# The rounding pass of the weights' high part on GpSimd in place of ScalarE

## The chip, the cores and the metric

One core of a Trainium2 chip runs the whole program: one launch, inputs and output in device memory. The metric is the device time of an execution in microseconds (us). The kernel before took 1209.21 us, the median of three runs (1208.96 to 1211.28).

## The reference

Top-k attention, then two feed-forward layers. All tensors are float32 except the weights, which are float64 (the draw is multiplied by a float64 scalar).

```python
scores = scale * q @ k^T                       # 4 batches, 8 heads, 576 tokens, 64 columns
kth = the 32nd largest of each row of scores
scores = where(scores >= kth, scores, -1e9)
attn = exp(scores - max) / (sum + 1e-9)
x = (attn @ v), heads side by side             # 2304 x 512
h = max(x @ w_in, 0);  x = (h * h) @ w_out     # 512 -> 2048 -> 512
h = x @ w_in2;  out = max(0.01 * h, h) @ w_out2
```

## The kernel before, in words

*Precision by parts.* TensorE multiplies values in a reduced 32-bit format (`R` in the code). To keep float32 accuracy the kernel splits a tensor into a high part, which is the value rounded to that format, and a low part, the value minus the high part. A product is then three matmuls: high by high, high by low, low by high. The helper `split_hi` (L111) makes a high part: with `act=True` on ScalarE, otherwise as one `tensor_scalar` on GpSimd that multiplies by 1.0 twice (L115). The low part is a `tensor_tensor` subtraction.

*Attention.* The 2304 tokens lie in nine units of 64 to 320 tokens; each unit has four head pairs, and the 128-row tiles of all of them go in 72 pairs of tiles through VectorE. For one pair VectorE alternates eight MAX8 (L829) and six MATCH_REPLACE8 (L831) to find the 32 largest of each row; then GpSimd makes the shifts `nb` (L288, L289), ScalarE the mask and the exponentials with their sums (L295, L299), GpSimd and VectorE the reciprocal (L303, L304), GpSimd the scaling of the rows (L308), TensorE the transposes (L313, L326) and the products with v (L397, L408). Score matmuls (L276) are evicted by ScalarE (L277).

*Feed-forward.* The tokens go in six blocks (512, 256, 384, 512, 256, 384). A block goes through a layer in 16 steps, one for each 128 columns of the hidden layer. Each step is 12 matmuls into `h` (L575), then the activation, which yields `gh` and `gl` (high and low part of the hidden values), and 12 matmuls into `acc` (L618 in the first layer, L620 in the second). The `acc` matmuls of a step come after the `h` matmuls of the next one (`LAG = 1`). In the first layer of block 0 the activation is relu and square on ScalarE (L585, L586), then on GpSimd the product L587 and the difference L601. In the second it is two relus on ScalarE (L596, L597), GpSimd's difference L598, ScalarE's `gh` (L600) and GpSimd's `gl` (L601).

*Weights.* A step uses a tile `wi` and a tile `wo`, each with a high and a low half of 128x512. Block 0 meets each of the 2 x 16 steps' weights for the first time and has to make them; it runs between about 180 and 445 us. Later blocks load the finished halves (`w_load`, L537, L538) from a copy in device memory that `w_store` (L529, L530) wrote. Making a tile (`w_convert_steps`): SP loads the raw float64 words (`w_raw`, L486, 4 buffers), ScalarE takes both 32-bit words to a scratch tile `wc` (4 buffers) and to a PSUM bank (L509, L510), VectorE joins them into the float32 value (L514, L515), ScalarE rounds it to the high half (L519), and GpSimd subtracts for the low half (L521). So 64 tiles, each with one L519 and one L521.

*Order.* The program is written out as a list of slots, 16 for each pair of attention tiles; each event (a load, a split, a score matmul) has a slot, and the feed-forward steps advance by portions between them, at a rate fixed for each block. A generator's `yield` ends a portion. While a step's matmuls are emitted, `next(conv, None)` emits one more portion of the conversion of the step after the next (`w_convert(si + 2)`): three times among the `h` matmuls, once behind the activation, four times among the `acc` matmuls; what is left over is emitted at the end of the step. `w_store(si + 1)` and `w_raw(si + 4)` stand at a step's start and end. The framework then orders the instructions by priority (events and conversions have a raised one) against its own model of the engines, puts in the semaphores, and each engine works its queue strictly in that order.

Of the kernel before, what the change touches and what calls it, by code (L numbers as in the profile page):

```python
# [11 lines left out]
AF = mybir.ActivationFunctionType  # L12
# [59 lines left out]
def topk_attention_moe_moe2_kernel(  # L72
# [21 lines left out]
    PE, ACT, DVE, POOL, SP = nc.tensor, nc.scalar, nc.vector, nc.gpsimd, nc.sync  # L94
# [6 lines left out]
    def bank():  # L101
        return psum.tile([P, 512], F, tag="att", name="att", bufs=3)
# [4 lines left out]
    def behind(key):  # L107

        return tc.issue_after(cur[key].ins) if key in cur else ExitStack()

    def split_hi(dst, src, act=False):  # L111
        if act:
            ACT.activation(dst, src, AF.Copy)
            return
        POOL.tensor_scalar(dst, src, 1.0, 1.0, op0=OP.mult, op1=OP.mult)  # L115
# [355 lines left out]
    def w_alloc(i):  # L471
        wi = pool.tile([P, 2, 512], R, tag="wi", name="wi", bufs=3)
        wo = pool.tile([P, 2, 512], R, tag="wo", name="wo", bufs=4)
        wt[i] = (wi, wo)
        return wi, wo
# [16 lines left out]
    def w_convert(i):  # L492
        g = w_convert_steps(i)
        while True:
            with tc.high_priority(offset=CONVP):
                if next(g, 1):
                    return
            yield

    def w_convert_steps(i):  # L500
        if i >= len(steps) or not fresh[i]:
            return
        w2 = w_alloc(i)
        for raw, w in zip(wraw.pop(i), w2):
            if W64:
                lo, hi = raw[:, :, 0], raw[:, :, 1]
                b = pool.tile([P, 512], U, tag="wc", name="wc", bufs=WCB)
                v = bank()
                ACT.activation(b, lo, AF.Copy, scale=L_SCALE, bias=L_BIAS)  # L509
                ACT.activation(v, hi.bitcast(F), AF.Copy, scale=H_SCALE)  # L510
                yield 0
                vu, c = v.bitcast(U), b.bitcast(F)
                with behind("dve"):
                    DVE.scalar_tensor_tensor(b, vu, 3, b, op0=OP.logical_shift_left, op1=OP.bitwise_or)  # L514
                DVE.scalar_tensor_tensor(b, vu, 0x80000000, b, op0=OP.bitwise_and, op1=OP.bitwise_or)  # L515
                yield 0
            else:
                c = raw
            ACT.activation(w[:, 0, :], c, AF.Copy)  # L519
            yield 0  # L520
            POOL.tensor_tensor(w[:, 1, :], c, w.bitcast(F)[:, 0, :], op=OP.subtract)  # L521
            yield 0

# [381 lines left out]
```

## Time and profile before

| what | value |
|---|---|
| median of three runs | 1209.21 us |
| the profiled execution | 1210.15 us, span 1208.4 us |
| TensorE matmul (PE) | busy 1135.8 us, 94% |
| VectorE (DVE) | busy 946.5 us, 78% |
| ScalarE (ACT) | busy 807.5 us, 67% |
| GpSimd (POOL) | busy 682.8 us, 57% |
| mean granted TensorE clock | 0.98 of full speed |

The profile is of one execution. Busy time leaves out register, branch, semaphore and DMA-issuing instructions. PEld is TensorE's weight load, which overlaps the matmuls. Lines (L519) are those of the kernel's file, where a helper's instructions have the helper's line. The shares are means over stretches with different limits, so most of what follows is read from one stretch.

### The profile page before, as it was taken

The page shows a single profiled execution, that of the slowest core. Times are in us where ns is not written, and L with a number is a line of the kernel's source. Part 1 is how long each engine was busy: PE and PEld are TensorE (multiplying, and loading weights), DVE is VectorE, ACT ScalarE, POOL GpSimd, SP SyncE. Part 2 cuts the span into 40 slices and gives each one's busy share as a digit, 9 for nine tenths or more (in the row PEclk, how much of TensorE's full clock was granted, in tenths as well). Part 3 has the DMA queues.
Part 4 walks back from the last instruction along what each step waited for, and adds up shares of the span by engine and source line. Part 5 has one row for each costly group of instructions (what it writes and reads, how often), then busy time and mean ns, then how long its engine had stood idle before and what let it go on. Part 6 is the DMA issues. An engine that isn't in the chain of part 4 may idle for free.

```text
span 1208.4 us, 20261 instructions
## 1 busy us (share of the span) xinstructions
PE 1135.8 (94%) x6388; PEld 992.5 (82%) x6388; DVE 946.5 (78%) x1944; ACT 807.5 (67%) x1831; POOL 682.8 (57%) x982
## 2 busy tenths in 40 slices
PE   4988987999889999999999999999999999999998
PEld 3776765887678779988999898888788899999997
DVE  7999899868988999999999999999999930110122
ACT  6988898878998986766656666555666653334322
POOL 7765564877878876556666665555565644004300
PEclk9899897999999999999999999999999999999999
DMA  9765566779989888879988888776676679779974
GB/s 307 255 217 192 192 220 222 267 233 333 342 280 319 305 267 263 296 269 384 355 293 290 298 272 286 221 227 226 201 239 211 199 255 369 253 253 341 356 256 135
DMA packets 110522, 323.25 MB, mean 268 GB/s; under 512 B 17488, under 2 KB 25680, under 8 KB 110416
## 3 DMA queue, kind: packets, MB, share of 16 engines
q1 hardware_dynamic: 107776, 317.24, 77.5%
q10 hardware_dynamic: 2640, 4.72, 1.1%
q8 instruction: 52, 0.85, 0.3%
q14 instruction: 54, 0.44, 0.1%
HBM read 254.54 MB, written 67.37 MB: 266 GB/s over the span
## 4 chain that ended last, share of the span: by engine, by line
PE 71%; ACT 11%; DVE 7%; DMA 6%; issue 2%; POOL 1%; ACTq 0%; SPq 0%; POOLq 0%; DVEq 0%
PE h L575 29%; PE acc L620 14%; PE acc L618 14%; PE att L408 4%; PE att L313 4%; DVE m L829 3%; PE att L397 3%; DVE w L831 3%; DMA wraw<-in_w_dram 2%; DMA sd<-stage 2%; ACT stage L277 1%; ACT e L299 1%; ACT e L295 1%; ACT s L277 1%; PE sp L276 1%
## 5 line engine op out<-in xcount | busy, mean ns | idle before, releaser
L575 PE MATMUL h<-xh,wi 128*128 128x512 f32 (+2 forms) x1280 | 349.9, 345 | 13.4 <-ACT gb L597 4.2
L829 DVE MAX8 m<-w 128x8 f32<-128x576 f32 x432 | 311.9, 748 | 1.1
L575 PEld LDWEIGHTS h<-xh,wi 128*128 128x128 f32 x1280 | 227.5, 191 | 42.6 <-ACT gb L597 5.8
L831 DVE MATCH_REPLACE8 w<-m,w 128x576 f32<-128x576 f32 x288 | 213.5, 744 | 0.8
L575 PE MATMUL h<-xl,wi 128*128 128x512 f32 (+2 forms) x640 | 207.6, 342 | 0.6 <-DVE xl L632 0.6
L601 POOL TENSOR_TENSOR gl<-ga,gh 128x512 fp32r<-128x512 f32 (+2 forms) x160 | 162.7, 1017 | 37.9 <-ACT gh L600 32.1
L618 PE MATMUL acc<-gh,wo 128*128 128x512 f32 (+2 forms) x768 | 156.8, 340 | 0.0
L620 PE MATMUL acc<-wo,gh 128*128 128x512 f32 x576 | 152.5, 399 | 2.9 <-ACT gh L600 2.7
L598 POOL TENSOR_TENSOR ga<-ga,gb 128x512 f32<-128x512 f32 (+2 forms) x80 | 81.4, 1017 | 130.6 <-ACT gb L597 127.3
L618 PEld LDWEIGHTS acc<-gh,wo 128*128 128x128 f32 x768 | 126.5, 189 | 11.0 <-ACT gh L586 0.2
L575 PEld LDWEIGHTS h<-xl,wi 128*128 128x128 f32 x640 | 121.4, 191 | 12.3 <-DVE xl L632 1.1
L295 ACT ACTIVATE e<-s,m 128x576 f32<-128x576 f32 x144 | 111.7, 779 | 18.6 <-DVE m L829 13.4
L620 PEld LDWEIGHTS acc<-wo,gh 128*128 128x128 f32 x576 | 104.3, 189 | 24.1 <-ACT gh L600 5.0
L829 DVE MAX8 m<-s 128x8 f32<-128x576 f32 x144 | 104.1, 748 | 12.5 <-ACT s L277 6.1
L299 ACT ACTIVATE e<-e,nb 128x576 f32<-128x576 f32 x144 | 111.0, 774 | 3.2 <-POOL nb L289 2.8
L587 POOL TENSOR_TENSOR ga<-ga 128x512 f32<-128x512 f32 (+2 forms) x80 | 66.1, 827 | 78.1 <-ACT gh L586 72.8
L831 DVE MATCH_REPLACE8 w<-m,s 128x576 f32<-128x576 f32 x144 | 107.1, 744 | 0.6
L313 PE MATMUL att<-ident,e 128*128 128x128 f32 x576 | 90.8, 281 | 13.7 <-ACT e L299 5.1
L313 PEld LDWEIGHTS att<-ident,e 128*128 128x128 f32 x576 | 70.0, 143 | 27.4 <-ACT e L299 10.1
L308 POOL TENSOR_SCALAR e<-e,rc 128x576 f32<-128x576 f32 x108 | 79.8, 749 | 22.5 <-DVE rc L304 21.1
L585 ACT ACTIVATE ga<-h 128x512 f32<-128x512 f32 (+2 forms) x80 | 39.0, 488 | 77.4 <-PE h L575 71.9
L618 PE MATMUL acc<-gl,wo 128*128 128x512 f32 (+2 forms) x384 | 87.7, 345 | 0.1
(94 smaller groups left out, 2136.7 us busy)
## 6 DMA issues: line engine op xcount, KB each, us to landing
wi<-wd SPq DMA_DIRECT2D x160, 512.0 KB, 5.0
wo<-wd SPq DMA_DIRECT2D x160, 512.0 KB, 5.2
wraw<-in_w_dram SPq DMA_DIRECT2D x64, 512.0 KB, 6.0
sd<-stage SPq DMA_DIRECT2D x72, 288.0 KB, 2.9
s<-sd SPq DMA_DIRECT2D x72, 288.0 KB, 4.6
wd<-wi SPq DMA_DIRECT2D x32, 512.0 KB, 5.4
wd<-wo SPq DMA_DIRECT2D x32, 512.0 KB, 5.9
kraw<-in_k_dram SPq DMA_DIRECT2D x16, 576.0 KB, 5.4
```

The costliest lines, as they stand in the source:

```text
L295: ACT.activation(t["e"], t["s"], AF.Prelu, bias=pr["m8"][:, i, 31:32], scale=-1.0, alpha=0.125 / FAR)
L299: ACT.activation(e, e, AF.Exp, bias=pr["nb"][:, i:i + 1], scale=-FAR, accum_out=pr["sum"][:, i:i + 1])
L308: POOL.tensor_scalar(e, e, pr["rc"][:, i:i + 1], 1.0, op0=OP.mult, op1=OP.mult)
L313: PE.transpose(ps[:, j * P:(j + 1) * P], t["e"][:, j * P:(j + 1) * P], ident)
L575: PE.matmul(h[:, 0:n], lhsT=wi[:, w, c * P:(c + 1) * P], rhs=x[c][y][:, 0:n], start=cnt == 0, stop=cnt == 3 * NK - 1)
L587: POOL.tensor_tensor(a[:, 0:n], a[:, 0:n], a[:, 0:n], op=OP.mult)
L598: POOL.tensor_tensor(a[:, 0:n], a[:, 0:n], b[:, 0:n], op=OP.subtract)
L601: (DVE if j >= GLD else POOL).tensor_tensor(gl[:, 0:n], a[:, 0:n], gh.bitcast(F)[:, 0:n], op=OP.subtract)
L618: PE.matmul(acc[c][:, 0:n], lhsT=wo[:, w, cs], rhs=g[:, 0:n], start=first, stop=last)
L620: PE.matmul(acc[c], lhsT=g[:, cs], rhs=wo[:, w, :], start=first, stop=last)
L829: cur["dve"] = DVE.max(out=m8[:, x, 8 * r:8 * r + 8], in_=t["s"] if r == 0 else t["w"])
L831: cur["dve"] = DVE.match_replace(out=t["w"], in_to_replace=m8[:, x, 8 * r:8 * r + 8], in_values=t["s"] if r == 0 else t["w"], imm_value=NEG)
```

## The change

The conversion's rounding pass calls the helper, which without `act` uses GpSimd. It stands directly in front of the subtraction that reads its result, and the `yield` between the two is gone, so that a tile's conversion has three portions and a step's six.

```diff
             else:
                 c = raw
-            ACT.activation(w[:, 0, :], c, AF.Copy)
-            yield 0
+            split_hi(w[:, 0, :], c)
             POOL.tensor_tensor(w[:, 1, :], c, w.bitcast(F)[:, 0, :], op=OP.subtract)
             yield 0
```

`split_hi(dst, src)` is `POOL.tensor_scalar(dst, src, 1.0, 1.0, op0=OP.mult, op1=OP.mult)`.

## Rows read from the trace of the kernel before

**Rows 1.** Windows, all engines: stretch, length, busy us (instructions), granted clock, DMA share, GB/s.
```profile
core 0: us, PE busy (x) PEld busy (x) DVE busy (x) ACT busy (x) POOL busy (x), PEclk, DMA share, GB/s
180.00:280.00 100.00, 91.67 (x440) 73.74 (x440) 83.24 (x165) 80.32 (x173) 65.88 (x76) 0.91 0.74 249
280.00:335.00 55.00, 45.35 (x205) 34.91 (x204) 48.41 (x93) 51.31 (x106) 43.49 (x49) 0.97 0.92 336
335.00:437.00 102.00, 99.30 (x479) 81.43 (x480) 89.05 (x166) 92.27 (x187) 88.57 (x92) 0.98 0.87 296
437.00:945.00 508.00, 499.06 (x2913) 445.28 (x2911) 499.77 (x1052) 326.22 (x723) 301.72 (x465) 0.99 0.80 270
945.00:1208.00 263.00, 256.30 (x1561) 240.08 (x1559) 60.66 (x119) 102.07 (x229) 63.88 (x91) 0.99 0.78 270
```
**Rows 2.** Windows, all engines, 280 to 437 us as one stretch.
```profile
280.00:437.00 157.00, 144.65 (x683) 116.34 (x683) 137.46 (x258) 143.58 (x293) 132.06 (x140) 0.98 0.89 310
```
**Rows 3.** Waits of PE, 280 to 437: waiter <- awaited, us, times, longest.
```profile
PE h L575 <- ACT gb L597: 3.4, 3, 2.2
PE h L575 <- ACT wi L519: 3.1, 2, 1.6
PE att L408 <- DVE PTs L336: 2.3, 2, 1.3
PE att L276 <- ACT s L277: 1.5, 1, 1.5
PE acc L620 <- ACT gh L600: 1.3, 1, 1.3
PE h L575 <- ACT ga L585: 0.6, 1, 0.6
```
**Rows 4.** Chain of waits (start us, us, what), and a window with the granted clock.
```profile
283.41 4.60 PE h L575 x12
...
334.96 4.57 PE h L575 x12
...
343.46 2.77 PE h L575 x12
...
284.00:286.00 2.00, 2.00 (x6) 1.52 (x6) 1.99 (x4) 2.00 (x5) 1.07 (x3) 0.50 1.02 416
```
**Rows 5.** ScalarE's line L519, 280 to 437: count, ns min/median/max, first and last start.
```profile
L519 ACT ACTIVATE wo<-wc x22: 616/624/663, 279.4 to 431.5; 128x512 fp32r<-128x512 f32 x22
L519 ACT ACTIVATE wi<-wc x21: 612/618/667, 282.7 to 429.2; 128x512 fp32r<-128x512 f32 x21
its engine sat idle before it (us, times) until:
  DVE wc L515: 1.5, 4
```
**Rows 6.** GpSimd's groups by shape: count | busy us, mean ns | idle before.
```profile
L115 POOL TENSOR_SCALAR q<-qraw 128x320 fp32r<-128x320 f32 x24 | 11.0, 458 | 24.5 <-PE sp L276 22.6 <-PE att L276 1.9
L115 POOL TENSOR_SCALAR KTa<-kraw 128x576 fp32r<-128x576 f32 x16 | 10.4, 670 | 1.9 <-DMA kraw<-in_k_dram 1.9
...
L521 POOL TENSOR_TENSOR wo<-wc,wo 128x512 fp32r<-128x512 f32 x32 | 41.5, 1295 | 5.5 <-ACT wo L519 5.2
```
**Rows 7.** GpSimd's timeline at two places: start us, us, instruction.
```profile
346.44 0.46 POOL L115 TENSOR_SCALAR q<-qraw 128x320 fp32r<-128x320 f32 x1 [0.86 <-PE att L276]
346.99 0.88 POOL L255 TENSOR_TENSOR q<-qraw,q 128x320 fp32r<-128x320 f32 x1
...
371.71 0.48 POOL L115 TENSOR_SCALAR q<-qraw 128x320 fp32r<-128x320 f32 x1
372.14 1.32 POOL L601 TENSOR_TENSOR gl<-ga,gh 128x512 fp32r<-128x512 f32 x1
```
**Rows 8.** Waits of GpSimd, 280 to 437.
```profile
POOL wi L521 <- ACT wi L519: 4.3, 3, 1.9
POOL sum L303 <- ACT e L299: 4.3, 4, 1.7
POOL ga L598 <- ACT gb L597: 3.8, 2, 2.7
POOL gl L601 <- ACT gh L600: 3.6, 4, 1.8
POOL e L308 <- DVE rc L304: 2.5, 4, 1.3
POOL ga L587 <- ACT gh L586: 2.5, 2, 2.2
POOL wo L521 <- ACT wo L519: 2.1, 4, 0.9
POOL q L115 <- PE att L276: 1.0, 2, 0.9
```
**Rows 9.** Waits of SP's DMA queue, 280 to 437.
```profile
SPq L529 <- POOL wi L521: 27.2, 16, 5.2
SPq L530 <- POOL wo L521: 15.2, 13, 3.8
```
**Rows 10.** Waits of VectorE and ScalarE on conversion lines, 280 to 437.
```profile
DVE wc L514 <- ACT att L510: 6.9, 7, 2.8
...
ACT wc L509 <- DMA wraw<-in_w_dram: 3.2, 2, 1.9
```
**Rows 11.** GpSimd's groups by line, 280 to 437.
```profile
L308 POOL TENSOR_SCALAR e<-e,rc 128x576 f32<-128x576 f32 x14 | 10.3, 748 | 2.6 <-DVE rc L304 2.5
L587 POOL TENSOR_TENSOR ga<-ga 128x512 f32<-128x512 f32 x6 | 6.2, 1039 | 2.5 <-ACT gh L586 2.5
```

## The prediction

> **What bounds the kernel now.** I read the profile in four steps: busy time by stretch, who waited for whom on TensorE, how the two engines of the change spend the stretch that has the conversions, and the queue of GpSimd instruction by instruction. All 64 rounding passes and their 64 subtractions lie between 180 and 437 us, so only that stretch can change by itself; everything behind it can only move. Behind it nothing has slack to give back or to soak up: from 437 to 945 VectorE is busy 500 of 508 us and TensorE 499, and from 945 to the end TensorE 256 of 263 [rows 1]. TensorE's whole work is fixed, so a shift of the end is the change of TensorE's idle time up to 437 us.
>
> The conversion stretch has two halves that differ. From 180 to 280 us nothing is full but TensorE, and GpSimd has 34 of 100 us free [rows 1]. From 280 to 437 us TensorE is busy 144.7 and ScalarE 143.6 of 157 us, 92% each, VectorE 88% and GpSimd 132.1, 84% [rows 2]. In its last 102 us TensorE is at 99.3: there it is the bound, with ScalarE (92.3) and GpSimd (88.6) close under it [rows 1]. TensorE's 12.4 us of idle in the 157 us are nearly all waits for ScalarE and VectorE: 3.4 for gb, 3.1 for the rounding pass L519 itself, 2.3 for PTs, 1.5 for a score eviction, 1.3 for gh, 0.6 for ga [rows 3]. After its longer pauses TensorE also runs some matmuls at the lower of its two clocks (granted share 0.50): twelve then take 4.60 and 4.57 us in place of 2.77 [rows 4].
>
> **The change, part by part.** *Removed from ScalarE:* 64 passes of 0.62 us, some 40 us in all; 43 of them between 280 and 437, 26.7 us [rows 5]. ScalarE falls there from 143.6 to 117 of 157 us and stops being near full. What is behind such a pass on its in-order queue comes earlier: the score evictions, relu, gh and the next tensor's two splitting passes.
>
> *Added to GpSimd:* 64 passes of 128x512, one input, from the helper at L115. The trace has this operation at 320 columns (458 ns) and 576 (670 ns) [rows 6]: 0.83 ns a column, so 512 columns take 670 - 64 x 0.83 = 617 ns. What one adds to a full queue is its start-to-start step. Ahead of an independent instruction a 0.48 us pass gave a step of 0.43 (371.71 to 372.14); ahead of the subtraction that needs it a 0.46 us pass gave 0.55 (346.44 to 346.99) [rows 7]. So 0.57 to 0.70 us each; I take 0.62, nearer to the first, because the scheduler may put another instruction between the two. Far bounds: 0.46 us (the 320-column row) and 1.30 us (the two-input row of the same 512 columns, L521) [rows 6]. Sum 64 x 0.62 = 39.7 us, of it 43 x 0.62 = 26.7 between 280 and 437.
>
> The Trainium skill, "GPSIMD Engine Reference", section 3.1, gives 769 ns as measured for 512 elements at its best-case loop of about 1.8 cycles an element, and elsewhere in that section 1.03 cycles for bodies of at most two operations. The rows' slope, 0.83 ns, is 1.0 cycle at the page's 1.2 GHz, so the trace sides with the second; by the first the 43 passes would be 33.1 us, 6.4 more than my sum.
>
> *The sum for GpSimd, 280 to 437:* 132.1 busy now plus 26.7 is 158.8 us of work in a stretch of 157. The earlier half stays under its length: 65.9 + 21 x 0.62 = 78.9 of 100. GpSimd cannot be busy without a gap. Its 24.9 us idle now are 6.4 for L519 itself (3 + 4 times), 14.2 for other ScalarE results (e, gb, gh), 2.5 for the reciprocal and 1.0 for a matmul [rows 8]. The first goes: the pass then waits for VectorE's L515, for which ScalarE idled only 1.5 us here [rows 5]. The reciprocal wait stays, a round trip from GpSimd to VectorE and back, and so does the 1.0: 3.5 us. Of the 14.2 I keep a quarter, 3.5, since a late engine finds its inputs ready and a lighter ScalarE delivers earlier. So 158.8 + 3.5 + 3.5 = 165.8 us for what takes 157: +8.8. Bounds of this term: with no gap and the 0.57 step, 156.6, nothing; with the 0.70 step and 92% busy, the best that any engine reaches in this stretch now, (132.1 + 30.1) / 0.92 = 176, +19.
>
> *What queues behind the added pass:* on GpSimd the products and differences L598 and L601, which release gh (by L600) and the last third of the second matmul group, the shifts nb that release the exponentials, and the sums that release the reciprocal. TensorE waited only 1.3 us for gh here, but it has just one hidden step of lag between the two layers' matmuls. On SP the stores L529 and L530 wait for the subtraction's result already, 27.2 + 15.2 us in this stretch [rows 9]; behind them stand the loads of the next raw weights, for which L509 waited 3.2 us [rows 10]. Each store comes later by what GpSimd is late.
>
> *Moved:* a conversion of two tensors is emitted in six portions, not eight, beside a matmul step that offers eight; so it ends a quarter of a step earlier, and 24 matmuls of 0.23 us (2.77 / 12) make 5.5 us, a quarter 1.4. It hides the pass's own latency, which is why I charge GpSimd's capacity and not its latency; without that cover, and with the subtraction's result needed at once, each step would pay 2 x 0.62.
>
> *Gain ahead of 280 us:* TensorE idles 8.3 us from 180 to 280 [rows 1], 22 rounding passes of ScalarE lie there, and ScalarE is 80% busy. I take 2 us, between 0 and 5.
>
> Net +8.8 - 2 = +6.8. The profiled execution took 1210.15 us (span 1208.4, 1.75 around it), 0.9 over the median of the runs, 1209.21; so 1216.95 for a profile and 1216 for the median. A measurement of this kernel tells 0.2%, 2.4 us, from no change.
>
> **Rivals.** *ScalarE was the pace-maker and its relief wins.* For it: the pass is in TensorE's waits by name (3.1 us), ScalarE's results end 9.9 of the 12.4 us of TensorE's idle in the stretch [rows 3], VectorE waits 6.9 us for L510 [rows 10], and each of two pauses cost another 1.8 us at the lower clock [rows 4]. Price at most 9.9 + 3.6 + 5 ahead of 280 = 18.5; TensorE's 99.3 of 102 leave little in the last part, so some 8: 1201. It decides if GpSimd's gaps shrink to almost nothing, that is if the stretch ends below 157 with GpSimd near 100%. Against it: 158.8 is more than 157.
>
> *No change.* GpSimd runs a few us behind through the stretch but the two-step lead of the weights absorbs it, and TensorE, 97% busy from 335 on, sets the pace as now: 1209.
>
> *The delay multiplies.* GpSimd at 92% as in the bound above, +19, and two more pauses with a lower-clock restart, 3.6, less the 2 ahead: some +17 to +21, 1228. It decides if L598 stands behind rounding and subtraction together (0.62 + 1.30 us), since then gh is late in every step.
>
> *The pass is slower than its helper's rows say.* The other one-input pass of GpSimd, L308, takes 748 ns at 576 columns, so some 0.69 us at 512, and L587, which multiplies a tile by itself, 1.04 us at 512 [rows 11]. At 0.69 the 43 passes add 3.3 us to my sum, at 1.04 18; the first row is much the nearer in kind: 1220. The skill's 769 ns, named above, would give 1222. It decides from the first pass on, and its row against it is L115's own.
>
> *That the change doesn't do what it says:* the scheduler may order the queues afresh, so that products go ahead of conversions; this moves the time either way by a pause or two, 2 to 5 us, and is in the ranges.
>
> **How the numbers follow.** Forecast case (slower by 3 to 13): 0.40. Relief wins: 0.23. No change: 0.20. Multiplied delay: 0.13. Slower pass: 0.04. Slower by over 0.2%: 0.40 + 0.13 + 0.04 = 0.57; within: 0.20; faster: 0.23. For the range I leave out half of the relief case below 1202 and some 0.06 of the multiplied delay above 1227; the forecast's own range is 1212 to 1222.
>
> **What would show it.** In the profile after: L115 with 64 more instructions near 617 ns and no L519 on ScalarE; GpSimd's busy time 39 us higher, ScalarE's 40 lower; GpSimd near 95% between 280 and the end of the conversions, and that end later by 5 to 10 us; TensorE's waits for gh and gl grown, those for s and gb shrunk; behind it the same distances as now. Wrong if the conversions end earlier than 437 us, if GpSimd keeps its gaps with TensorE at its old pace, or if the shift arises behind 437.

## The result and the profile after

The changed kernel takes 1219.91 us, the median of 7 runs (1216.54 to 1224.18), against 1209.50 for the kernel before (7 runs): 0.83% slower, ratio 1.0083, 95% interval 1.0068 to 1.0098. The forecast was 1216 with 1202 to 1227. The profiled execution has a span of 1220.5 us, 12.1 more than before.

The busy times did what the diff says. This is the page's first part for the changed kernel (busy us, share of the span, instructions):

```profile
span 1220.5 us, 20225 instructions
PE 1140.9 (93%) x6388; PEld 995.3 (82%) x6388; DVE 946.4 (78%) x1944; ACT 777.5 (64%) x1767; POOL 720.2 (59%) x1046
```

ScalarE has 64 instructions and 30 us less (807.5 before), GpSimd 64 more and 37.4 us more (682.8). I had written 40 for both: the 64 passes do last 40 us, but where two instructions overlap at their ends busy time counts once. TensorE's span grew by 7.0 us of idle and 5.1 us of busy time with the same 6388 matmuls; the second part goes with a lower mean granted clock (0.977 against 0.980).

Next, the windows of the changed kernel that answer to [rows 1] and [rows 2], the last three cut at the later end of the conversions (stretch, length, then busy us of PE, PEld, DVE, ACT, POOL; granted clock, DMA share, GB/s):

```profile
180.00:280.00 100.00, 90.66 (x420) 73.39 (x419) 82.19 (x163) 68.15 (x149) 74.39 (x95) 0.88 0.70 238
280.00:335.00 55.00, 45.42 (x206) 34.87 (x205) 49.62 (x96) 42.95 (x88) 53.42 (x67) 0.94 0.93 341
335.00:437.00 102.00, 93.00 (x423) 74.98 (x424) 83.48 (x155) 75.86 (x154) 94.09 (x109) 0.95 0.80 280
...
280.00:447.00 167.00, 148.42 (x683) 118.41 (x683) 139.31 (x262) 122.73 (x250) 157.50 (x184) 0.95 0.83 293
447.00:957.00 510.00, 501.05 (x2934) 445.94 (x2933) 501.46 (x1053) 330.89 (x729) 306.09 (x469) 1.00 0.80 272
957.00:1220.00 263.00, 257.34 (x1564) 240.72 (x1562) 58.82 (x117) 101.24 (x226) 63.20 (x89) 1.00 0.77 269
```

GpSimd is now the fullest engine: 53.4 of 55 us, and 157.5 of the 167 that TensorE needs for the same 683 matmuls as before in 157 [rows 2]. ScalarE fell to 122.7 of 167. Behind 447 us nothing changed but the position: 2934 and 1564 matmuls where there were 2913 and 1561, in windows of 510 and 263 us in place of 508 and 263. So in this execution the whole loss was made by 447 us. Some of it lies ahead of 280 us, where TensorE got through 420 matmuls in place of 440 at a clock of 0.88 in place of 0.91.

The new instructions (the helper's line from 280 to 447 us in groups: count | busy us, mean ns | idle before, releaser) and the place where GpSimd stood still for one of them (timeline: start us, us, instruction, idle before it):

```profile
L115 POOL TENSOR_SCALAR wo<-wc 128x512 fp32r<-128x512 f32 x22 | 13.8, 629 | 0.0
L115 POOL TENSOR_SCALAR wi<-wc 128x512 fp32r<-128x512 f32 x21 | 13.2, 628 | 5.2 <-PE h L574 4.9
```

```profile
343.64 1.28 POOL L520 TENSOR_TENSOR wo<-wc,wo 128x512 fp32r<-128x512 f32 x1
349.86 0.62 POOL L115 TENSOR_SCALAR wi<-wc 128x512 fp32r<-128x512 f32 x1 [4.94 <-PE h L574]
350.56 1.28 POOL L520 TENSOR_TENSOR wi<-wc,wi 128x512 fp32r<-128x512 f32 x1
351.93 0.19 POOL L303 TENSOR_SCALAR sum<-sum 128x2 f32<-128x2 f32 x1
```

The pass takes 0.63 us. From its start to the start of the next instruction it is 0.58 us (the median of 40 of these 43 passes, which have another instruction between them and their subtraction) and 0.70 us in the three that have not, as in the one shown. Once the pass stood 4.9 us at the head of GpSimd's queue, because the `wi` tile that it writes was still being read by TensorE. A sum for the attention (L303) stood behind it, but the last exponentials that it adds up ended only at 350.2 us, so the wait held up the conversion more than the attention. Last, TensorE's waits from 280 to 447 us, which answer to [rows 3] (us in total, times, longest):

```profile
PE acc L619 <- ACT gh L599: 5.2, 4, 2.4
PE att L276 <- DVE wc L515: 2.7, 2, 1.9
PE att L313 <- DVE wc L515: 2.5, 1, 2.5
PE h L574 <- ACT ga L584: 2.1, 2, 1.7
PE att L313 <- DVE PTs L319: 1.9, 1, 1.9
PE h L574 <- ACT xh L630: 1.5, 3, 0.5
```

The wait for gh went from 1.3 to 5.2 us. The wait for L515 is new: score matmuls and transposes wait for a PSUM bank of the tag `att`, which a conversion holds from L510 until VectorE has read it. It is not of the moved pass alone: e1 below, with GpSimd's load as before, has 2.3 us of it. The waits for the rounding pass itself (3.1) are gone.

### The profile page after: what moved, and what is told of

It is laid out like the page before. It is cut to its first block, busy times and chain, and to the rows that moved or that the text cites. A ratio compares the mean times of both kernels' runs of the same rounds, so it can differ in the third digit from the quotient of the medians.

```text
span 1220.5 us, 20225 instructions
## 1 busy us (share of the span) xinstructions
PE 1140.9 (93%) x6388; PEld 995.3 (82%) x6388; DVE 946.4 (78%) x1944; ACT 777.5 (64%) x1767; POOL 720.2 (59%) x1046
## 4 chain that ended last, share of the span: by engine, by line
PE 75%; ACT 9%; DVE 7%; DMA 3%; POOL 2%; issue 2%; ACTq 0%; POOLq 0%; DVEq 0%
PE h L574 30%; PE acc L619 15%; PE acc L617 15%; PE att L408 4%; PE att L313 4%; PE att L397 4%; DVE m L828 3%; DVE w L830 2%; DMA sd<-stage 2%; PE att L276 1%; ACT e L295 1%; ACT stage L277 1%; ACT e L299 1%; PE sp L276 1%; ACT s L277 1%
## 5 line engine op out<-in xcount | busy, mean ns | idle before, releaser
L295 ACT ACTIVATE e<-s,m 128x576 f32<-128x576 f32 x144 | 112.3, 781 | 27.6 <-DVE m L828 22.8
```

Of the source, the lines that this page charges most:

```text
L295: ACT.activation(t["e"], t["s"], AF.Prelu, bias=pr["m8"][:, i, 31:32], scale=-1.0, alpha=0.125 / FAR)
```

## The experiments

Each was timed beside the kernel before on its chip (medians there: 1209.39 for the first four, 1210.37 for the next four, 1209.00 for the last four). For the profiled execution of each I also took three things that tell where the time went: how late the reciprocals (L304) of the tile pairs 28 to 57 start against the kernel before, as a mean (negative: ahead of it), and TensorE's idle time (length less busy) in two windows. Those windows, for the kernel before and the changed one:

```profile
180.00:460.00 280.00, 257.45 (x1257) 209.58 (x1257) 243.21 (x468) 241.70 (x507) 212.96 (x243) 0.95 0.83 284
460.00:945.00 485.00, 477.92 (x2778) 425.78 (x2776) 477.25 (x1006) 308.43 (x679) 286.69 (x437) 1.00 0.80 271
```

```profile
180.00:460.00 280.00, 251.55 (x1167) 202.24 (x1166) 234.11 (x448) 200.18 (x418) 242.19 (x297) 0.93 0.78 271
460.00:945.00 485.00, 476.58 (x2809) 425.44 (x2809) 477.24 (x1006) 313.61 (x692) 289.06 (x441) 1.00 0.81 273
```

So 22.6 and 7.1 us idle before, 28.4 and 8.4 after. All kernels (the shift and the idle columns are of one execution each):

| kernel | median us | ratio to before, 95% | pairs 28-57 late by | PE idle 180-460 | PE idle 460-945 |
|---|---|---|---|---|---|
| before | 1209.5 | 1 | 0 | 22.6 | 7.1 |
| changed | 1219.9 | 1.0083 (1.0068 to 1.0098) | 11.1 | 28.4 | 8.4 |
| e1: boundary out, pass on ScalarE | 1215.5 | 1.0041 (1.0026 to 1.0055) | 3.4 | 22.4 | 9.1 |
| e2: boundary kept, pass on GpSimd | 1214.1 | 1.0036 (1.0022 to 1.0049) | 4.5 | 26.7 | 7.0 |
| e3: a pass on both | 1214.1 | 1.0039 (1.0024 to 1.0054) | 5.7 | 27.6 | 7.1 |
| e4: no pass | 1212.1 | 1.0020 (1.0006 to 1.0035) | -4.5 | 21.9 | 11.2 |
| n5: boundary elsewhere | 1219.0 | 1.0080 (1.0058 to 1.0102) | 0.8 | 22.9 | 14.8 |
| n4: one boundary more | 1220.1 | 1.0081 (1.0067 to 1.0096) | 0.3 | 22.3 | 13.7 |
| d1: two passes on GpSimd | 1245.4 | 1.0290 (1.0273 to 1.0306) | 30.4 | 41.3 | 11.6 |
| d2: two passes on ScalarE | 1231.0 | 1.0171 (1.0157 to 1.0184) | 16.9 | 29.9 | 12.1 |
| f1: GpSimd for ten steps | 1207.8 | 0.9990 (0.9979 to 1.0002) | -9.7 | 15.9 | 10.7 |
| f2: GpSimd for the others | 1216.1 | 1.0052 (1.0035 to 1.0068) | -1.2 | 25.9 | 8.1 |

**e1, the boundary alone.**

```diff
             ACT.activation(w[:, 0, :], c, AF.Copy)
-            yield 0
```

> The kernel before with only the portion boundary between rounding and subtraction taken out; the rounding stays on ScalarE. Theory (GpSimd's work in the stretch from 280 us to the end of the conversions exceeds the time): no GpSimd work is added, so 1207 to 1212 us, GpSimd busy 683 us as before. Rival (the earlier emission and the new order of the queues that it makes cost the time): 1216 to 1224 us, like the changed kernel, with GpSimd's busy time unchanged.

1215.54 us, 6.1 over the kernel before, with GpSimd's load unchanged (682.8 us): between the two ranges, close to the rival's. So the removed `yield`, which the forecast held to be harmless, costs more than half of what the whole change costs. TensorE's idle is as before (72.3 us in all against 72.6); its busy time is 5.7 us longer, at a mean granted clock of 0.974 against 0.980. The conversions are not late: the last subtraction starts at 434.6 us, 0.6 earlier than before.

**e2, the pass alone.**

```diff
-            ACT.activation(w[:, 0, :], c, AF.Copy)
+            split_hi(w[:, 0, :], c)
             yield 0
```

> The changed kernel with the portion boundary kept: rounding on GpSimd, then the end of a portion, then the subtraction. Theory of GpSimd's capacity: the same 40 us of work on GpSimd, so 1215 to 1224 us, GpSimd again over 92% busy between 280 us and the end of the conversions. Rival of emission and order: back to 1207 to 1212 us.

1214.13, 4.7 over the kernel before; just under the range of my theory, clearly over the rival's. GpSimd is as full as the theory says, 96.97 of 102 us in the second of these windows:

```profile
280.00:335.00 55.00, 43.88 (x201) 34.13 (x199) 49.33 (x96) 40.08 (x82) 52.86 (x66) 0.95 0.89 327
335.00:437.00 102.00, 95.59 (x443) 76.62 (x444) 83.33 (x155) 77.80 (x159) 96.97 (x111) 0.96 0.81 287
```

The last subtraction starts at 439.2 us, 4 later than before (435.2). The two parts add up: 6.1 + 4.7 = 10.8, measured together 10.4.

**e3, both passes.**

```diff
             ACT.activation(w[:, 0, :], c, AF.Copy)
+            POOL.tensor_scalar(scr, c, 1.0, 1.0, op0=OP.mult, op1=OP.mult)   # 128x512 scratch
             yield 0
```

> The kernel before with its rounding on ScalarE kept, and beside it the same pass on GpSimd into a scratch tile, in front of the subtraction: GpSimd has the load of the changed kernel, ScalarE that of the kernel before. Theory of GpSimd's capacity, with ScalarE's relief worth 2 to 3 us: 1219 to 1226 us. Rival (ScalarE's relief is worth much, some 8 us, and hides a loss on GpSimd of twice what is seen): 1227 to 1235 us. Rival of order: anything, no relation to the load.

1214.09, the same as e2: with GpSimd loaded, giving ScalarE its passes back cost nothing. Below both ranges. That fits an engine that sets the pace alone, but by itself it doesn't separate load from order.

**e4, no pass.**

```diff
-            DVE.scalar_tensor_tensor(b, vu, 0x80000000, b, op0=OP.bitwise_and, op1=OP.bitwise_or)
+            DVE.tensor_tensor(w[:, 0, :], v, c, op=OP.add)
...
-            ACT.activation(w[:, 0, :], c, AF.Copy)
-            yield 0
```

> Neither engine has the rounding pass: VectorE's second joining instruction is a floating-point add of the same size that writes the rounded high half itself (the sign bit is left out, so the weights are not the reference's). Theory of GpSimd's capacity with a small relief of ScalarE: 1203 to 1209 us. Rival (ScalarE was the pace-maker, its relief is worth some 8 us or more): 1195 to 1202 us. Rival of order: 1212 or more.

1212.06, slightly slower than before although ScalarE lost its 64 passes and no engine gained any: a miss for my theory and for the relief, a hit at the edge for the order. But the edit takes the boundary out too, as e1 does; against e1 (1215.54) it is 3.5 us faster, so it does not say what ScalarE's relief is worth by itself. The attention did run 4.5 us ahead, and TensorE lost it again behind 460 us (11.2 us idle against 7.1).

**n5 and n4, the same work in other portions.** That called for cuts that change no engine's work.

```diff
             ACT.activation(b, lo, AF.Copy, scale=L_SCALE, bias=L_BIAS)
+            yield 0
             ACT.activation(v, hi.bitcast(F), AF.Copy, scale=H_SCALE)
...
             ACT.activation(w[:, 0, :], c, AF.Copy)
-            yield 0                      # in n5; n4 keeps this one
```

> The kernel before with its portions cut elsewhere: no boundary between rounding and subtraction, one between ScalarE's two splitting passes instead, so eight portions a step as before. No engine's work changes. Theory of GpSimd's capacity alone, and the theory that the number of portions (how early a conversion is emitted) costs the 6 us seen when one was taken out: 1207 to 1212 us. Rival (any new order of the queues costs a few us against this one): 1212 to 1218 us.

> The kernel before with one portion boundary more, between ScalarE's two splitting passes: ten portions a step, of which two are emitted at the step's end. No engine's work changes. Theory of the number of portions (fewer is dearer): 1204 to 1210 us. Rival (any new order costs a few us): 1212 to 1218 us.

1218.97 and 1220.09: 8.6 and 9.7 us slower with the same instructions, both above the rival's range. It is not the number of portions, since six, eight and ten of them all cost. What is left is the new order that the framework makes of every queue. The loss lies elsewhere than in the changed kernel: the attention is on time, TensorE idles 22.9 and 22.3 us up to 460, as before, and 14.8 and 13.7 behind it. In n5 one stretch holds most, here beside the wait in it:

```profile
700.00:760.00 60.00, 51.07 (x280) 45.11 (x278) 58.97 (x125) 36.96 (x82) 31.90 (x49) 0.96 0.79 260
...
PE att L313 <- POOL e L308: 4.7, 1, 4.7
```

The kernel before has TensorE busy for 57.99 us there and 0.7 for that wait. So a comparison of two orders of this program carries up to 10 us that no engine's load explains, and the total alone can't say what a pass costs.

**d1 and d2, the pass twice.**

```diff
-            ACT.activation(w[:, 0, :], c, AF.Copy)
+            split_hi(w[:, 0, :], c);  split_hi(scr, c)          # d1
+            ACT.activation(w[:, 0, :], c, AF.Copy);  ACT.activation(scr, c, AF.Copy)   # d2
             yield 0
```

> Rounding on GpSimd, its portion boundary kept, and the same pass a second time on GpSimd into a scratch tile: twice the added load, none on ScalarE. Theory of GpSimd's capacity: 132.1 + 2 x 26.7 = 185.5 us of work from 280 us on where the kernel before needed 157, so some 25 to 38 us over the kernel before, 1234 to 1248 us. Rival of order: 1211 to 1220 us, as with one pass.

> The kernel before with the rounding pass twice on ScalarE, the second time into a scratch tile: 64 passes more on ScalarE, none on GpSimd. ScalarE's work from 280 us on becomes 143.6 + 26.7 = 170 us where the kernel before needed 157. If ScalarE is as close to full as its busy time says: 13 to 25 us over the kernel before, 1222 to 1235 us. Rival of order: 1211 to 1217 us.

d1: 1245.35, 35.0 over the kernel before where e2 is 4.7 over it, so 30 us for 64 passes more: here the load speaks far over any order. GpSimd is busy 98.87 of 102 us, and TensorE's idle up to 460 is 41.3 us. From 280 us to the end of the last subtraction at 472.3 GpSimd has 187.7 us of work, where the expectation had 185.5, in 192.3 us:

```profile
335.00:437.00 102.00, 87.75 (x383) 67.06 (x383) 74.34 (x136) 68.00 (x136) 98.87 (x121) 0.95 0.76 259
280.00:472.30 192.30, 160.93 (x713) 124.07 (x712) 145.70 (x267) 129.21 (x260) 187.69 (x232) 0.96 0.77 264
```

d2: 1231.03, 20.7 over. ScalarE is close to full too (99.4 of 102 us from 335 on in d2, 92.3 before), so the kernel before stands between two engines that both have little room; taking work from one and giving it to the other can only gain where the second has some.

**f1 and f2, where the pass falls.**

```diff
-            ACT.activation(w[:, 0, :], c, AF.Copy)
+            split_hi(w[:, 0, :], c, i >= 10)     # f1: GpSimd for ten steps;  f2: i < 10, GpSimd for the others
             yield 0
```

> Rounding on GpSimd for the first ten steps (20 tiles, converted up to about 280 us, where GpSimd had a third of its time free), on ScalarE for the other 44 tiles; the portion boundary kept. Theory of GpSimd's capacity: the attention of the tile pairs 28 to 57 runs within 2 us of the kernel before or up to 3 us ahead, since the passes fall where GpSimd has room. Rival (a pass on GpSimd costs wherever it stands, by the wait of what is behind it): 1 to 2 us behind, a third of what all 64 passes cost there (4.6). Total time by the scatter that new orders of the queues showed (0 to 10 us behind the conversions): 1207 to 1219 us.

> The other way round: ScalarE rounds for the first ten steps, GpSimd for the other 44 tiles, from about 280 us on; the portion boundary kept. Theory of GpSimd's capacity: the whole loss of the 64 passes is in these 44, so pairs 28 to 57 run 4 to 7 us late, GpSimd over 93% busy from 280 us to the end of the conversions. Rival (a pass costs wherever it stands): two thirds, some 3 us. Total 1211 to 1222 us.

f1: 1207.84 against 1209.00, not told apart from the kernel before, though inside the conversion stretch it is far better than I expected: the attention runs 9.7 us ahead and TensorE idles 15.9 us in place of 22.6. Of these 6.7 us TensorE gives back 3.6 behind 460 (10.7 idle against 7.1); the profiled span is 1203.9, 4.5 under, but that is the fastest of its 12 executions. The gain lies behind 280 us, not ahead of it: TensorE idles 8.7 us from 180 to 280 (8.3 before) with the same 440 matmuls, 6.1 from 280 to 335 (9.7) and 0.7 from 335 to 437 (2.7). What came earlier ahead of 280 is VectorE's work, 87.0 us of it against 83.2:

```profile
180.00:280.00 100.00, 91.28 (x440) 73.78 (x439) 86.97 (x174) 74.36 (x162) 78.50 (x100) 0.93 0.76 258
280.00:335.00 55.00, 48.92 (x230) 39.21 (x231) 51.27 (x98) 51.66 (x106) 47.41 (x50) 0.97 0.97 355
335.00:437.00 102.00, 101.31 (x504) 83.95 (x503) 89.17 (x170) 93.85 (x196) 90.43 (x100) 1.00 0.87 295
```

f2: 1216.05, 7.0 slower, with TensorE idle up to 460 at 25.9 and GpSimd nearly full:

```profile
280.00:335.00 55.00, 44.85 (x211) 35.61 (x210) 52.16 (x102) 43.09 (x88) 53.50 (x67) 0.94 0.97 348
335.00:437.00 102.00, 95.60 (x456) 76.76 (x455) 87.66 (x166) 79.92 (x164) 97.93 (x112) 0.98 0.79 281
```

That fits the capacity, by which the place of the pass decides; the totals alone, 8.2 us apart, would not show it beside orders that scatter by up to 10. But the pairs 28 to 57 were on time in f2, not 4 to 7 us late as I had written: there it is the feed-forward that fell behind (1235 matmuls from 180 to 460 us, 1257 before). The lateness of the attention is not a safe gauge of the loss; TensorE's idle time is a better one, though e1's loss is not in it.

**p0 and p1, ordered by priority alone.**

```diff
-    with _tile.TileContext(nc, schedule_with_timeline_sim=True) as tc:
+    with _tile.TileContext(nc, schedule_with_timeline_sim=False) as tc:     # p0; p1 has e2's edit besides
```

> The kernel before, ordered by priorities alone and not against the framework's model of the engines. Its time is only a base for the next run; no theory forecasts it. Guess: 1210 to 1260 us.

> The same order by priorities alone, rounding on GpSimd, portion boundary kept; against the run just before far fewer places of the queues differ than between the kernel before and the changed one. Theory of GpSimd's capacity with a loss of 4 to 8 us that is its own: 4 to 8 us over that run. Rival (the loss is the scatter of new orders and the moved load costs nothing that can be measured): within 2.5 us of that run.

1307.99 and 1323.01: the pass costs 15 us on this base, more than either theory said. Against p0 the last subtraction of p1 starts 13.7 us later (483.5 against 469.7), and from the pair 49 on each reciprocal is 14.4 to 14.8 us late, so nothing behind the conversions added or gave back anything. The base is another kernel, 99 us slower; its 15 us are no measure of the cost in the tuned order. The loss is there in a second order too, but how far re-cuts scatter on this base wasn't measured.

## Why the prediction was right, and where it wasn't

**What bounds the kernel: right for the conversion stretch, wrong for what follows.** "Everything behind it can only move" holds for the changed kernel (the windows from 447 us on) and fails for n5, n4, e4 and f1, in which TensorE lost 4 to 8 us more behind 460 us than before. The framework orders the whole program anew, and a wait of 4.7 us can then appear behind 700 us for an edit whose instructions all lie ahead of 437. Nor is "a shift of the end is the change of TensorE's idle time" right: 5.1 of the 12.1 us are in its busy time, and in e1 all of it.

**The added pass: right.** 0.62 us a pass forecast, 0.63 measured, and 0.58 from start to start in most of them; so the "slower pass" rival is out, and with it the 769 ns of the Trainium skill ("GPSIMD Engine Reference", section 3.1); the trace agrees with that section's rate for bodies of at most two operations.

**The sum for GpSimd: right for the changed kernel, too large for the pass alone.** The forecast had 158.8 us of work and 7 of gaps, so an end at 445.8 us. In the changed kernel the last subtraction ends at 447.2, with 157.7 us of work and 9.5 of gaps. In size both agree; but 4.9 of the gaps are the one wait for a `wi` tile, which I didn't have, and of the waits for ScalarE, for which I had kept 3.5, 1.9 are left. With the boundary kept (e2) the stretch ends at 440.5, 4 us later than before and not 8.8. The gaps are 7.2 there, as forecast; it is the work that is less, 153.3 us, because some of it fell outside the stretch: 41 passes lie in it where the sum and the changed kernel have 43, two more having run ahead of 280 us, where GpSimd has room, and 40 products and differences of the feed-forward in place of the 42 before (changed kernel, then e2 twice):

```profile
280.00:447.20 167.20, 148.62 (x685) 118.61 (x685) 139.51 (x262) 122.93 (x250) 157.70 (x184) 0.95 0.82 292
...
180.00:280.00 100.00, 91.50 (x444) 74.25 (x443) 86.35 (x171) 72.80 (x159) 78.95 (x100) 0.93 0.73 253
280.00:440.50 160.50, 142.97 (x664) 113.87 (x663) 135.77 (x255) 119.43 (x244) 153.32 (x179) 0.96 0.83 297
```

The sum held the work after 280 us fixed, and that was its weak term. The total of e2, +4.7, is near to its +4; with orders that scatter by up to 10 us this agreement is not proof. What shows the load is where TensorE waits: 25.9 to 28.4 us idle up to 460 in the four kernels with one pass on GpSimd from 280 us on, 21.9 to 22.9 in five that leave GpSimd's load there as it was and have none or one on ScalarE (before, e1, n5, n4, e4) and 15.9 in the sixth (f1), 41.3 with two; and the step of 30 us from e2 to d1.

**"Moved": this is the step that failed.** I took the portion that was dropped for a cover that ends a conversion earlier and costs nothing. Taking it out costs 6.1 us with the pass on ScalarE (e1) and 5.7 with the pass on GpSimd (10.4 for the changed kernel, less 4.7 for e2). The two need not be the same thing. In e1 the conversions end on time and TensorE's busy time is longer. In the changed kernel GpSimd stood idle for longer than in e2, 25.6 us against 21.1 from 180 to 280 and 9.5 against 7.2 behind it, and the last subtraction starts 6.7 us later. The 4.9 us wait for the `wi` tile is not the boundary's own: with the boundary kept, e2 and f2 have such a wait too, only shorter (GpSimd's waits from 280 us on, e2 and then f2):

```profile
POOL wi L115 <- PE h L575: 2.3, 1, 2.3
POOL wi L115 <- PE h L575: 3.4, 1, 3.4
```

n5 and n4 show that a new cut as such costs as much; which part of the 6 us belongs to the earlier emission and which to the order stays open. A fourth `wi` buffer, which might take that wait away, wasn't tried.

**The gain ahead of 280 us: not there.** TensorE idled 9.3 us from 180 to 280, 1.0 more than before, at the lower clock named above. f1, which has the passes of this part on GpSimd and the others on ScalarE, idles 8.7 us there, no less than before either; its 6.7 us less up to 460 come behind 280 us.

**The rivals.** Relief wins: in f1 alone, up to 460 us, and in sum not measurable. No change: no. The delay multiplies: its price (+17 to +21) was not reached, its two signs are there: the wait for gh rose to 5.2 us and TensorE's busy time by 5.1 us, with more matmuls at the lower clock. The wait for a PSUM bank held by a conversion (5.2 us; 8.9 in e2) was in no case of mine. Mine in sum: +8.8 - 2 = +6.8; the runs: about +5 for the pass and +6 for the boundary, 10.4 together. The net was nearer than its terms, and to that extent it was luck: what I had put too high for the pass made up for part of what I had put at nothing for the boundary.

## What to carry to other kernels

Add the work that moves to the busy time of its new engine in the stretch where it falls, not over the whole run: 59% over the span was 97% from 280 to 335 us. In a program whose queues a framework orders by a model, first time one or two cuts that change no work: here they moved the time by 6 to 10 us, and a difference of that size is then explained only by where the waits are, or by doubling the suspected cost. A dropped `yield` is an edit of its own and wants its own run.

## What the runs showed of the hardware that I had not expected

How much of a loss can sit in busy time. In the changed kernel TensorE stood 2.6 of 4 us from 312 on, among them 1.9 for the new wait on L515, and then ran 6 us at a granted clock of 0.52, which is the lower of its two levels, 1.2 GHz, for nearly all of it (windows as above; then the chain of waits: start us, us, what):

```profile
312.00:316.00 4.00, 1.39 (x7) 0.88 (x8) 4.00 (x9) 1.39 (x3) 4.00 (x6) 0.87 0.67 235
316.00:322.00 6.00, 6.00 (x17) 4.66 (x18) 5.93 (x12) 2.50 (x6) 6.00 (x8) 0.52 0.71 238
```

```profile
305.87 2.80 PE acc L617 x12
...
316.67 5.12 PE acc L617 x12
```

Twelve matmuls then took 5.12 us in place of 2.80, so the pause cost nearly twice its length. In e1 busy time is the whole loss as far as the profile shows it: idle no longer than before, busy time 5.7 us longer. Over all runs the mean clocks bear this out only loosely: 0.973 to 0.982 in e1's five, 0.979 to 0.987 in those of the kernel before on that chip.
